# RWKV6 attention and an MLP mixer: the first batch in a fixed order, with more zero products on TensorE

## The chip, the core and the metric

The kernel runs on one core of one Trainium2 chip. The engines that matter are TensorE (PE: matmul; its weight loads are listed as PEld), VectorE (DVE), ScalarE (ACT), GpSimd (POOL) and SyncE (SP), which issues nearly all DMAs. The metric is device time in microseconds, the median of several executions. Everything is float32.

## The reference

For each batch (B = 4), head (H = 8) and time step t (S = 768 steps, head dimension D = 48), the attention keeps a 48 x 48 state:

```
y[t]  = r[t] @ (state + outer(u * k[t], v[t]))
state = w[t][:, None] * state + outer(k[t], v[t])
```

The heads' outputs, side by side, are x of shape (4, 768, 384). The mixer then mixes over tokens and over channels:

```
h   = relu(x^T @ w_tok1) @ w_tok2        # w_tok1 768 x 256, w_tok2 256 x 768
u   = x + h^T
out = u + relu(u @ w_ch1) @ w_ch2        # w_ch1 384 x 1536, w_ch2 1536 x 384
```

The weights come in as 64-bit floats, and the kernel turns them into float32 itself.

## The kernel before, in words

**Attention.** The work is cut into twelve units, three for each batch; a unit is 256 tokens of all heads. Two heads lie on top of each other in the partitions (P = 64 rows each, 48 of them used), and A = 4 such pairs and UC = 2 chunks of 128 tokens lie along the free dimension. Within blocks of 64 tokens the decayed products of r and k are built level by level. `levels(i)` does this for unit i. Its piece `begin` makes copies of r and k with u applied (ScalarE, L195 and L199). `first_block` multiplies in the first decays (`join`, L250 to L252, VectorE), makes the first products on TensorE (`gram0`, L211) and picks the entries that are wanted out of PSUM (`pick0`, L217). `block(l)`, for levels 1 to 5, makes the products (`gram`, L225), joins, and picks (`pick`: VectorE at L234 for levels 1 to 3, ScalarE at L242 for 4 and 5). r and k are changed in place, so a join waits for the gram of its own level, and the next gram waits for the join. The products go to a PSUM pool of two buffers (`ps_g`).

`post(i)` finishes a unit. `tokens(c)` transposes k (L284), `carry(c)` makes the outer products of k and v (L296) and moves the state on by two blocks (L303 to L306), `before(c)` applies r to the states (L318) and `within(c)` adds the products inside the blocks (L331) and copies the result to x (L334). `carry`, `before` and `within` use the one buffer of `ps_a` in turn. The last two pieces load the inputs of unit i + 3 (`load_rkw`, L101, and `load_v`, L108): r, k and w lie in three sets of buffers.

**Weights.** `convert` (L142) loads a piece of a weight matrix as 64-bit words (L149, two buffers), takes the magnitude of the high words on ScalarE (L155) and puts the float32 together in six steps on VectorE (L156 to L161). There are 3 pieces of w_tok1 and 9 of w_ch1, 512 wide, and 4 of w_tok2 and 12 of w_ch2, 384 wide.

**Mixer.** `mixing(bt)` gives the pieces of a batch: `hidden` (L353, two sums that are open over all six chunks), `back` (L360, added to x at L362), `turn` (transposes, L367), `up` (L375, relu at L377) and `down` (L384, sum at L388, then the store at L389). They use the two buffers of `ps_m`. For the first batch `down` of the first segment is cut into pieces of two columns of weights each, with both sums open at once.

**Order.** Pieces are functions with an assumed cost. `woven` merges lists of them by their share of cost done, and `emit` calls them in turn. What a piece emits is then put in order by the framework, which plans each engine's queue by its own estimate of when instructions become ready, with the order of emission as priority: an instruction that is ready may be planned ahead of one that was emitted earlier. So pieces of batch 1 can stand in a queue between those of batch 0.

Of the kernel before, what the change touches and what calls it, by code (L numbers as in the profile page):

```python
# [10 lines left out]
f32 = mybir.dt.float32  # L11
# [31 lines left out]
    return [(c, f) for *_, c, f in sorted(keyed, key=lambda e: e[:3])]  # L43


def emit(pieces):
    for _, f in pieces:
        f()


@with_exitstack
def rwkv6_then_mixer(
    ctx: ExitStack,
# [20 lines left out]

    nc = tc.nc
    pe, dve, act, pool, sp = nc.tensor, nc.vector, nc.scalar, nc.gpsimd, nc.sync

    const = ctx.enter_context(tc.tile_pool(name="const", bufs=1))
    wts = ctx.enter_context(tc.tile_pool(name="wts", bufs=1))
# [29 lines left out]

    u_col = const.tile([128, A], f32, name="u_col")  # L110
    act.dma_start(u_col, u)
    load_rkw(0)
    load_rkw(1)

    masks = []
    for l in range(4):
        b = 1 << l
        m = const.tile([128, 64 // b, 2 if l == 0 else b], f32, name=f"mask{l}")  # L120
        pool.memset(m, 1.0)
        pool.affine_select(out=m, in_=m, compare_op=ALU.is_ge, fill=0.0, base=0,
                           pattern=[[-2 * b, 64 // b], [0, m.shape[2]]], channel_multiplier=1)
        pool.affine_select(out=m, in_=m, compare_op=ALU.is_ge, fill=0.0, base=b - 1,
                           pattern=[[2 * b, 64 // b], [1 if l == 0 else 0, m.shape[2]]], channel_multiplier=-1)
        n, x = (T, 1) if l == 0 else (32, UC * A)
        m8 = const.tile([128, x, n], u8, name=f"mask8_{l}")
        flat = m.rearrange("p n b -> p (n b)")
        for j in range(2):
            dve.tensor_copy(m8[ts(j, T)], flat[ts(j, T), ts(j, n)].unsqueeze(1).to_broadcast([T, x, n]))  # L130
        masks.append(m8)
    for i, t in enumerate(weights_at):
        (dve if i == 0 else pool).memset(t, 0.0)
    ident = const.tile([128, 128], f32, name="ident")
    make_identity(nc, ident)

# [38 lines left out]
    def levels(i):  # L175
# [94 lines left out]
    def post(i):  # L270
# [4 lines left out]
        def tokens(c):  # L275
            if half == 0 and c == 0:
                xs[bt] = xpool.tile([128, C, DM], f32, name="x")
            L = live[i]
            if bt == 0:
                ps = ps_g.tile([128, 2, 512], f32, name="gram")[:, 0, :].rearrange("p (a t) -> p a t", a=A)  # L280
            else:
                ps = ps_m.tile([128, A, 128], f32, name="kT_ps", tag="m")
            for a in range(A):
                pe.transpose(ps[:, a, :], k_[:, ts(c * A + a, 128)], ident)  # L284
            L["kT"] = apool.tile([128, A, 128], f32, name="kT")
            act.copy(L["kT"], ps)

        def carry(c):
            L, vt = live[i], vs[i]
            ch = half * UC + c  # L290
            last = ch == C - 1
            kv = ps_a.tile([128, 2, 512], f32, name="kv_ps", tag="a")
            for a in range(A):
                for j, q in ((0, 0), (1, 1), (0, 1), (1, 0)):
                    if not (last and j == 1):
                        pe.matmul(kv[ts(q, P), j, ts(a, D)], L["kT"][ts(j, T), a, ts(q, P)],  # L296
                                  vt[ts(j, T), c, ts(2 * a + q, D)], start=True, stop=True)
            for j in range(1 if last else 2):
# [173 lines left out]
```

## Time and profile before

| | us |
|---|---|
| median of 3 runs | 690.39 (689.81 to 694.6) |
| the profiled execution | 687.6 |
| its span, first to last instruction | 685.6 |
| PE busy | 641.6 (94%) |
| DVE busy | 293.1 (43%) |
| ACT busy | 194.8 (28%) |

The costliest groups are the channel mixing's two products: L375 203.2 us and L384 198.6 us of PE, followed by the grams at L225, 85.2 us. One matmul of the program is two records in the profile. Busy time of a group overlaps with its neighbours at the edges, and ends of matmuls are modelled. In a timeline row the columns are start, duration, engine, line, operation, output <- inputs, tile sizes and count; in brackets stands the idle time of the engine before it and what ended it. A row can stand for several instructions in a run.

### The profile page before, as it was taken

How to read it: one execution, taken by the hardware profiler on the slowest of the kernel's cores; microseconds unless marked ns; L12 is line 12 of the kernel's file. 1: busy time of each engine (PE TensorE's matmuls, PEld its weight loads, DVE VectorE, ACT ScalarE, POOL GpSimd, SP SyncE). 2: the span in 40 equal slices, each digit the busy share in tenths (PEclk: the TensorE clock that was granted, in tenths of full speed). 3: DMA queues.
4: the chain of work that ended last, by engine and by line, in shares of the span. 5: the costliest groups of instructions: out<-in, count | busy, mean ns of one | idle time of the engine just before them, and what ended most of it. 6: DMA issues, size and time to landing. Idle time of an engine off the chain costs nothing.

```text
span 685.6 us, 18835 instructions
## 1 busy us (share of the span) xinstructions
PE 641.6 (94%) x8584; PEld 466.9 (68%) x8584; DVE 293.1 (43%) x585; ACT 194.8 (28%) x489; POOL 7.2 (1%) x32
## 2 busy tenths in 40 slices
PE   3889998996799999999999999999999999999998
PEld 3877656863586666788677656788677655786854
DVE  5998899998821435442242305442132211000000
ACT  7144533441242123432321303432211201220200
POOL 3000000000000000000000000000000000000000
PEclk9997898998899999999999999999999999999999
DMA  9244544332202131110210312000000000000000
GB/s 345 69 107 132 146 140 126 124 115 71 70 25 81 36 95 48 25 25 5 80 35 3 94 35 60 2 2 2 13 13 2 25 12 12 1 0 12 12 16 31
DMA packets 16111, 38.56 MB, mean 56 GB/s; under 512 B 2176, under 2 KB 8320, under 8 KB 16032
## 3 DMA queue, kind: packets, MB, share of 16 engines
q1 hardware_dynamic: 15888, 37.36, 17.9%
q8 instruction: 67, 1.10, 0.7%
q14 instruction: 12, 0.10, 0.0%
q10 hardware_dynamic: 144, 0.00, 0.0%
HBM read 32.64 MB, written 4.72 MB: 54 GB/s over the span
## 4 chain that ended last, share of the span: by engine, by line
PE 87%; DVE 9%; issue 2%; ACT 1%; DMA 1%; SPq 0%; DVEq 0%; ACTq 0%
PE z_ps L375 29%; PE h_ps L384 28%; PE gram L225 9%; PE h_ps L353 5%; PE h_ps L360 5%; PE y_ps L331 4%; PE kv_ps L296 2%; PE y_ps L318 2%; DVE r L251 1%; DVE k L250 1%; PE kT_ps L284 1%; PE gram L211 1%; PE xT_ps L367 1%; DVE at L217 1%; DMA w<-in_rkw_dram 1%
## 5 line engine op out<-in xcount | busy, mean ns | idle before, releaser
L375 PE MATMUL z_ps<-xT,wch 128*128 128x256 f32 x864 | 203.2, 389 | 3.5 <-DVE wch L161 3.0
L384 PE MATMUL h_ps<-wch,z 128*128 128x384 f32 x576 | 198.6, 498 | 3.7 <-DVE wch L161 3.5
L375 PEld LDWEIGHTS z_ps<-xT,wch 128*128 128x128 f32 x864 | 161.4, 192 | 28.4 <-DVE wch L161 3.2
L384 PEld LDWEIGHTS h_ps<-wch,z 128*128 128x128 f32 x576 | 107.9, 192 | 73.1 <-DVE wch L161 3.7
L377 ACT ACTIVATE z<-z_ps 128x256 f32<-128x256 f32 x144 | 55.1, 383 | 177.3 <-PE z_ps L375 177.2
L225 PEld LDWEIGHTS gram<-r,k 48*64 48x64 f32 x3840 | 76.5, 152 | 34.7 <-issue 24.3
L225 PE MATMUL gram<-r,k 48*64 48x32 f32 x3840 | 85.2, 235 | 13.1 <-DVE r L251 8.5
L388 DVE TENSOR_TENSOR o<-x,h_ps 128x384 f32<-128x384 f32 x24 | 13.3, 554 | 181.9 <-PE h_ps L384 181.9
L250 DVE TENSOR_TENSOR k<-k,decay 112x512 f32<-112x512 f32 x36 | 24.9, 691 | 62.2 <-PE gram L225 62.2
L242 ACT COPY at<-gram 16x256 f32<-16x256 f32 (+1 forms) x72 | 31.2, 434 | 44.7 <-PE gram L225 37.3
L250 DVE TENSOR_TENSOR k<-k,w 112x512 f32<-112x512 f32 x36 | 24.8, 688 | 39.6 <-PE gram L225 32.9
L360 PE MATMUL h_ps<-h,wtok 128*128 128x384 f32 x96 | 36.0, 503 | 1.8 <-DVE x L362 1.8
L353 PE MATMUL h_ps<-x,wtok 128*128 128x384 f32 x96 | 37.0, 520 | 0.0
L331 PEld LDWEIGHTS y_ps<-vt,at 64*64 64x64 f32 x768 | 26.2, 142 | 9.9 <-ACT seen L324 6.3
L234 DVE COPY_PREDICATED at<-mask,gram 128x512 f32<-128x512 uint8 x36 | 32.3, 897 | 0.0
L251 DVE TENSOR_TENSOR r<-r,w 112x512 f32<-112x512 f32 x36 | 24.7, 686 | 16.5 <-ACT rp L195 16.5
L331 PE MATMUL y_ps<-vt,at 64*64 64x48 f32 x768 | 29.2, 227 | 2.1 <-ACT seen L324 1.8
L211 PE MATMUL gram<-rp,kp 48*64 48x64 f32 x768 | 20.1, 246 | 11.1 <-ACT kp L199 8.0
L211 PEld LDWEIGHTS gram<-rp,kp 48*64 48x64 f32 x768 | 17.1, 154 | 16.4 <-ACT kp L199 10.4
L217 DVE COPY_PREDICATED at<-mask,gram 128x512 f32<-128x512 uint8 x24 | 16.7, 725 | 25.7 <-PE gram L211 25.4
L155 ACT ACTIVATE size<-d 128x384 f32<-128x384 f32 (+1 forms) x28 | 17.0, 608 | 28.2 <-DMA d<-in_w_ch_dram 13.3
L324 ACT COPY seen<-y_ps 64x2 f32<-64x2 f32 x44 | 6.8, 154 | 63.6 <-PE y_ps L318 63.3
(50 smaller groups left out, 429.1 us busy)
## 6 DMA issues: line engine op xcount, KB each, us to landing
vt<-in_v_dram SPq DMA_DIRECT2D x12, 384.0 KB, 3.9
d<-in_w_ch_dram SPq DMA_DIRECT2D x9, 512.0 KB, 3.6
d<-in_w_ch_dram SPq DMA_DIRECT2D x12, 384.0 KB, 3.0
out_dram<-o SPq DMA_DIRECT2D x24, 192.0 KB, 1.9
w<-in_rkw_dram SPq DMA_DIRECT2D x18, 192.0 KB, 3.5
k<-in_rkw_dram SPq DMA_DIRECT2D x18, 192.0 KB, 3.5
r<-in_rkw_dram SPq DMA_DIRECT2D x18, 192.0 KB, 3.4
r<-in_rkw_dram SPq DMA_DIRECT2D x3, 512.0 KB, 6.1
```

The source lines that it names most:

```text
L211: pe.matmul(g[cols, q, ts(a, T)], L["kp"][rows, tokens], L["rp"][rows, tokens], start=True, stop=True)
L225: fours(lambda q, j, rows, cols: pe.matmul(g[cols, q, ts(ca, 32)], k_[rows, ds(ca * 128 + j * T, T)], right[rows, ts(2 * ca + j, 32 // b), ...
L234: dve.copy_predicated(out=dst, data=g.rearrange("p q (m b) -> p q m b", b=b), mask=masks[l].rearrange("p x t -> p (x t)").rearrange("p (m ...
L242: act.copy(at[p:p + b, :, :, n * 2 * b + b:(n + 1) * 2 * b], g[p:p + b, :, :, ts(n, b)])
L250: dve.tensor_mul(left, left, wv[:, :, 1].unsqueeze(2).to_broadcast([ROWS, n, b]))
L251: dve.tensor_mul(right, right, wv[:, :, 0].unsqueeze(2).to_broadcast([ROWS, n, b]))
L331: pe.matmul(y[ts(j, T), q, ts(a, D)], at[ts(j, T), q, c * A + a, :], vt[ts(j, T), c, ts(2 * a + q, D)], start=(2 * ch + j == 0 and a == A ...
L353: pe.matmul(sums[i], wtok1[:, c, ts(i, 128)], xs[bt][:, c, :], start=(c == 0), stop=(c == C - 1))
L360: pe.matmul(ps, wtok2[:, i, ts(c, 128)], h1[:, i, :], start=(i == 0), stop=(i == DTOK // 128 - 1))
L375: pe.matmul(ps, wch1[:, m, ts(jt, 128)], xT[:, m, ts(s, SEG)], start=(m == 0), stop=(m == DM // 128 - 1))
L377: act.activation(zs[s][:, jt, :], ps, AF.Relu)
L384: pe.matmul(ps, zs[s][:, jt, ts(n, 128)], wch2[:, jt, :], start=(jt == 0), stop=(jt == NJ - 1))
```

## The change

The first batch, with its attention, weight conversions and token mixing up to most of the first `down`, is emitted with `fixed=True`. `emit` then ties each instruction of PE, DVE, ACT and SP to the one emitted before it on the same engine, so that the framework can't plan it elsewhere; POOL isn't tied. Instructions emitted later without `fixed` are tied behind the last fixed one of their engine, and free among themselves.

The first batch's order is a list: the levels of its three units (a, b, c) start one after the other and alternate; `busy(n)` stands between them, n products of a zeroed part of the wtok2 buffer with itself, 128 x 128 by 256 columns, whose result nobody reads. Then come the pieces of `post`, the hidden pieces and the conversions of w_tok1 and of half of w_tok2, one by one. Updating the states is a piece of its own (`update`), behind the transposes of the next chunk. The loads of units 3 to 5 (`p0[10:]`, `p1[10:]`, `p2[10:]`) are emitted after token mixing and the third piece of w_ch1. The masks are made in one fixed piece ahead of everything, in two shared buffers, and the memset of the first weights_at buffer belongs to that piece. `touched` is a small ScalarE operation at the start; `decay` has three buffers. The diff, cut where it says nothing more:

```diff
-def emit(pieces):
-    for _, f in pieces:
-        f()
...
+    last = {}
+
+    def emit(pieces, fixed=False):
+        for _, f in pieces:
+            done = len(block.instructions)
+            f()
+            for ins in block.instructions[done:]:
+                if ins.engine in (pe.engine, dve.engine, act.engine, sp.engine):
+                    if ins.engine in last:
+                        tc.add_manual_dep(ins, last[ins.engine], behind, reason="order of the pieces")
+                    if fixed:
+                        last[ins.engine] = ins.name
...
+    touched = const.tile([1, 2], f32, name="touched")
+    dve.memset(touched, 0.0)
+    act.mul(touched[:, 1:], touched[:, :1], touched[:, :1])
     load_rkw(0)
     load_rkw(1)
...
+            m = wide.tile([128, 512], f32, name="size", bufs=2)[:, :64 // b * width].rearrange("p (n b) -> p n b", b=width)
...
+    emit([(0, make_masks)], fixed=True)
...
-            decay = apool.tile([128, COLS // 2], f32, name="decay")
+            decay = apool.tile([128, COLS // 2], f32, name="decay", bufs=3)
...
-        pieces = []
-        for c in range(UC):
-            pieces += [(0.5, lambda c=c: tokens(c)), (0.5, lambda c=c: carry(c))]
+        pieces = [(0.5, lambda: tokens(0)), (0.5, lambda: carry(0)), (0.5, lambda: tokens(1)), (0.1, lambda: update(0)),
+                  (0.5, lambda: carry(1)), (0.1, lambda: update(1))]
...
-    emit(woven(levels(0), levels(1)))
-    load_v(0)
     load_rkw(2)
-    load_v(1)
-    load_v(2)
+    for i in range(3):
+        load_v(i)
+
+    def busy(n):
+        ps = ps_m.tile([128, 256], f32, name="busy", tag="m")
+        for _ in range(n):
+            pe.matmul(ps, wtok2[:, 0, :128], wtok2[:, 0, :256], start=True, stop=True)
+
+    dve.memset(wtok2[:, 0, :256], 0.0)
+    a, b, c = levels(0), levels(1), levels(2)
     p0, p1, p2 = post(0), post(1), post(2)
-    p1[4:4] = hiddens[0] + hiddens[1]
-    p2[4:4] = hiddens[2] + hiddens[3]
-    emit(woven(levels(2), p0 + p1, to_tok1))
-    emit(woven(p2[:-4], to_tok2[:2]))
-    emit(p2[-4:-2] + hiddens[4] + p2[-2:] + hiddens[5])
+    begin = [e.pop(0) for e in (a, b, c)]
+    h, t1, t2 = hiddens, to_tok1, to_tok2
+    order = [begin[0], 12, begin[1], a[0], 2, a[1], 2, b[0], 2, a[2], 1, b[1], 2, begin[2], a[3], 2, b[2], 2, c[0], 2,
+             a[4], 2, b[3], 2, c[1], 2, a[5], 2, b[4], 1, c[2], 1, p0[0], b[5], 1, p0[1], c[3], p0[2], p0[3], 1,
+             p0[4], p0[5], 1, p0[6], c[4], p0[7], t1[0], p1[0], p0[8], c[5], p0[9],
+             p1[1], p1[2], *h[0], p1[3], p1[4], *h[1], p1[5], p2[0], p1[6], t1[1], p1[7], p2[2], p1[8], p1[9],
+             p2[1], p2[3], *h[2], p2[4], p2[5], *h[3], p2[6], t1[2], p2[7], p2[8], p2[9], t2[0], *h[4], t2[1], *h[5]]
+    emit([(0.4 * e, lambda e=e: busy(e)) if isinstance(e, int) else e for e in order], fixed=True)
...
-            emit(woven(turned, to_tok2[2:] + to_ch1[:3]))
+            emit(woven(turned, to_tok2[2:] + to_ch1[:3]) + p0[10:] + p1[10:] + p2[10:], fixed=True)
             both = [f for e in zip(ups[0], ups[1]) for f in e]
-            emit(woven(both, to_ch1[3:] + to_ch2[:6]))
-            emit(woven(downs[0][:-4], to_ch2[6:]))
+            emit(woven(both, to_ch1[3:] + to_ch2[:6]), fixed=True)
+            emit(woven(downs[0][:-4], to_ch2[6:]), fixed=True)
```

More of the change, by code (lines that the diff above doesn't have):

```diff
@@ L76, in rwkv6_then_mixer @@
     pe, dve, act, pool, sp = nc.tensor, nc.vector, nc.scalar, nc.gpsimd, nc.sync
+    block = nc.cur_bb.bb
+    behind = mybir.DependencyInfo(mybir.DependencyClass.NoSync, mybir.DependencyReason.DATA)
+    last = {}
[9 more added lines that the diff above has]
+                        last[ins.engine] = ins.name
     const = ctx.enter_context(tc.tile_pool(name="const", bufs=1))
@@ L117, in rwkv6_then_mixer, with make_masks @@
     masks = []
[L118 to L133, printed above, removed]
+    def make_masks():
+        for l in range(4):
+            b = 1 << l
+            width = 2 if l == 0 else b
+            m = wide.tile([128, 512], f32, name="size", bufs=2)[:, :64 // b * width].rearrange("p (n b) -> p n b", b=width)
+            pool.memset(m, 1.0)
+            pool.affine_select(out=m, in_=m, compare_op=ALU.is_ge, fill=0.0, base=0,
+                               pattern=[[-2 * b, 64 // b], [0, width]], channel_multiplier=1)
+            pool.affine_select(out=m, in_=m, compare_op=ALU.is_ge, fill=0.0, base=b - 1,
+                               pattern=[[2 * b, 64 // b], [1 if l == 0 else 0, width]], channel_multiplier=-1)
+            n, x = (T, 1) if l == 0 else (32, UC * A)
+            m8 = const.tile([128, x, n], u8, name=f"mask8_{l}")
+            flat = m.rearrange("p n b -> p (n b)")
+            for j in range(2):
+                dve.tensor_copy(m8[ts(j, T)], flat[ts(j, T), ts(j, n)].unsqueeze(1).to_broadcast([T, x, n]))
+            masks.append(m8)
+        for i, t in enumerate(weights_at):
+            (dve if i == 0 else pool).memset(t, 0.0)
+    emit([(0, make_masks)], fixed=True)
     ident = const.tile([128, 128], f32, name="ident")
@@ L284, in tokens @@
                 pe.transpose(ps[:, a, :], k_[:, ts(c * A + a, 128)], ident)
-            L["kT"] = apool.tile([128, A, 128], f32, name="kT")
-            act.copy(L["kT"], ps)
+            L["kT", c] = apool.tile([128, A, 128], f32, name="kT")
+            act.copy(L["kT", c], ps)
         def carry(c):
@@ L291, in carry @@
             last = ch == C - 1
-            kv = ps_a.tile([128, 2, 512], f32, name="kv_ps", tag="a")
+            kv = L["kv"] = ps_a.tile([128, 2, 512], f32, name="kv_ps", tag="a")
             for a in range(A):
@@ L295, in carry, with update @@
                     if not (last and j == 1):
-                        pe.matmul(kv[ts(q, P), j, ts(a, D)], L["kT"][ts(j, T), a, ts(q, P)],
+                        pe.matmul(kv[ts(q, P), j, ts(a, D)], L["kT", c][ts(j, T), a, ts(q, P)],
                                   vt[ts(j, T), c, ts(2 * a + q, D)], start=True, stop=True)
-            for j in range(1 if last else 2):
+        def update(c):
+            L = live[i]
+            ch = half * UC + c
+            kv = L.pop("kv")
+            for j in range(1 if ch == C - 1 else 2):
                 g = 2 * ch + j
```

## The prediction

> **What bounds the kernel now.** I read the table of stretches first, then TensorE's and VectorE's timelines inside the first 186 us, then the chain and the DMA landings. The stretches (columns: us, then busy us and instruction count of PE, PEld, DVE, ACT, POOL, then granted clock, DMA share, GB/s):
>
> ```profile
> 0.00:38.40 38.40, 24.60 (x772) 22.86 (x772) 29.37 (x57) 18.67 (x46) 6.32 (x24) 1.00 0.57 204
> 38.40:85.30 46.90, 41.90 (x1090) 33.32 (x1090) 40.82 (x91) 21.34 (x55) 0.33 (x3) 0.85 0.45 124
> 85.30:108.00 22.70, 17.78 (x253) 11.40 (x252) 21.93 (x43) 9.13 (x20) 0.00 (x0) 0.97 0.39 123
> 108.00:147.00 39.00, 38.99 (x186) 31.20 (x186) 36.41 (x71) 14.87 (x35) 0.00 (x0) 0.93 0.45 133
> 147.00:185.90 38.90, 27.84 (x595) 17.89 (x594) 34.49 (x72) 8.99 (x19) 0.00 (x0) 0.87 0.24 71
> 185.90:254.00 68.10, 66.75 (x878) 47.48 (x874) 20.48 (x45) 19.13 (x50) 0.33 (x3) 1.00 0.23 63
> ```
>
> Up to 185.9 us VectorE is the full engine (163 of 186 us); afterwards TensorE has no gap worth naming and VectorE is below a third. So the total is: TensorE's work, plus what TensorE loses before 186 us. What paces the early part is weight conversion, six dependent VectorE steps:
>
> ```profile
> 112.12 0.42 DVE L156 TENSOR_SCALAR cut<-d 128x512 uint32<-128x512 uint32 x1
> ...
> 115.29 0.69 DVE L161 SCALAR_TENSOR_TENSOR wch<-size,scale 128x512 f32<-128x512 f32 x1
> 115.90 0.42 DVE L156 TENSOR_SCALAR cut<-d 128x512 uint32<-128x512 uint32 x1
> ```
>
> One 512-wide conversion back to back is 115.90 - 112.12 = 3.78 us; a 384-wide one, read the same way (131.01 to 134.12), is 3.11 us. TensorE's timeline shows it waiting for them, and what its clock does:
>
> ```profile
> 27.46 3.89 PE L225 MATMUL gram<-r,k 48*64 48x32 f32 x128 [0.37 <-DVE at L234]
> ...
> 100.59 1.14 PE L225 MATMUL gram<-r,k 48*64 48x32 f32 x64 [0.22 <-DVE r L251]
> ...
> 108.01 13.28 PE L375 MATMUL z_ps<-xT,wch 128*128 128x256 f32 x48 [2.34 <-DVE wch L161]
> 123.09 10.63 PE L375 MATMUL z_ps<-xT,wch 128*128 128x256 f32 x48
> ...
> 156.00 1.56 PE L384 MATMUL h_ps<-wch,z 128*128 128x384 f32 x4 [2.10 <-DVE wch L161]
> ```
>
> Sixty-four gram records take 1.95 us at 27 us and 1.14 at 100: TensorE is slow in the first 40 us although the clock column says 1.00 there. And in 75 to 186 us the queues carry grams (L211, L225) of batch 1 between the conversions of batch 0: VectorE's form groups give 12 first-level picks (L217) and 32 left products (L250) before 190 us, where batch 0 alone needs 6 and 18.
>
> **What the Trainium skill says.** "TensorE: Matmul & The Clock Gate", Part 1: the array runs at half clock until a 3.4 us window has been busy, and falls back after an idle one. The trace agrees (1.95 against 1.14 us; 0.50 granted between 48.6 and 55.3 us) and adds that a stream of small grams, 93% busy in the records from 25 to 35 us, does not release it. "PSUM — Partial Sum Buffer", Engine vs sequencer instructions: the queues of ScalarE and VectorE are strict FIFO, so a fixed order is what runs, stalls included; nothing in this trace contradicts it, though none of its rows tests it. "DMA: Bandwidth & Descriptors", Queues, rings and completion order: each engine consumes a ring in order. The trace's start agrees: 6.95 MB were queued, and landings grow with position.
>
> ```profile
> r<-in_rkw_dram SPq DMA_DIRECT2D x3, 512.0 KB, 6.1
> k<-in_rkw_dram SPq DMA_DIRECT2D x3, 512.0 KB, 6.9
> w<-in_rkw_dram SPq DMA_DIRECT2D x3, 512.0 KB, 7.6
> vt<-in_v_dram SPq DMA_DIRECT2D x3, 384.0 KB, 9.8
> d<-in_w_tok_dram SPq DMA_DIRECT2D x2, 512.0 KB, 11.0
> ```
>
> A lone weight load of 512 KB takes 3.6 us.
>
> **The change, part by part.** Call the attention units of batch 0 a, b, c; a level is a gram, two products (L250, L251: 1.20 us by start-to-start), the next decay (0.6 down to 0.1) and a pick (1.22, 1.08, 0.6, 0.6; the last two on ScalarE). A unit is 12.2 us of VectorE.
>
> *Masks, memset, table load.* The mask casts (8 instructions, 2.2 us of VectorE at 8.4 to 11.6) move ahead of the first product, into VectorE's idle time up to 7.16 us; the memset (0.9) moves behind them, so the first product starts at about 7.9. Worth -1.5 us. POOL's mask work now shares two buffers and so waits for a cast or two (0.3 us each); it ended at 6.4 us, so this stays in the same idle time. The table load, at 1.23 us already, was hidden by the first DMA: 0. load_v(0) goes behind load_rkw(2) on SP: a first use at 46 us hides it. The third decay buffer: 0, what it lets start earlier stands behind other work in the fixed order.
>
> *Products of zeros.* One is two records of 256 columns: 10.63/48 = 0.22 each, 0.44 us warm, 0.85 cold. Twelve while the first loads arrive, from about 1.5 us: five to seven cold, the rest warm, ending at 8.5 to 9.7, against a first gram at 7.96 now; that gram then takes 1.5 instead of 2.3 us, so 0 net. The other 28 are 12.4 us of TensorE warm. Between 30 and 45 us TensorE's own sum (five grams of 1.2, products 4.9 us, a transpose) is as long as VectorE's, so here they are partly on the path.
>
> *Levels.* Grams have two buffers, freed by picks, and the order is fixed, so I wrote it out piece by piece: a1 must wait for its gram with nothing behind it (1.45 us), b0's second gram waits for a1's pick, a4, b3, c2 and b5 wait 0.4 to 1.3 us each. Through the third level of c that is 30.7 us of VectorE plus 6 of waits: 7.9 + 36.7 = 44.6. Before, at 46.6 us, VectorE had done two units, c's first products, unit 0's states and a conversion. So no gain.
>
> *Posts.* carry, before and within share one accumulator (kv_ps, y_ps). A unit is twice (kv 0.66, update 4 x 0.39, release 0.2) and twice (y 0.68, seen 0.4, within 1.1, copy 0.55): 10.3 us. From 46: unit 0 takes 14.5 because c3 to c5 stand between, unit 1 11, unit 2 to its last update 4.7: 76.2. Behind that, in VectorE's order, stand t1[2], t2[0], t2[1] (3.78 + 2 x 3.11): the first back() at X = 86.2. Now it is at 85.4. Bounds: 82 (no wait beyond data) to 91 (half clock returns in the posts).
>
> *Token mixing.* VectorE's fixed order: first back 1.7, two wtok2 conversions 6.2, three wch1 11.3, six additions of 0.5: 22.2. The third wch1 conversion ends at 108.4; now at 107.96.
>
> *The moved loads.* load_rkw(3..5) and load_v(3..5) leave the posts and stand in SP's order behind the load of wch1's third piece, ahead of its fourth: 18 x 192 KB + 3 x 384 KB = 4.72 MB. The page gives 37.36 MB in 17.9% of the span, 304 GB/s: 15.5 us. They start when wch1's first piece has been read (X + 12.4 = 98.6), drain at 114.1, and the fourth piece behind them lands at 117.7 (1.7 for itself, 1.9 fixed); it is wanted at 108.4. Stall 9.3; at the 410 GB/s of the start 4.9; 0 if the queue doesn't hold it back. I take 8. Queued behind it: all later conversions on VectorE, and on ScalarE the abs (L155) of that piece with the relus of the ups after it, so TensorE too.
>
> *Conversions.* Six of wch1 and twelve of wch2 follow with nothing between: 22.7 + 37.3 = 60.0. The last ends at 108.4 + 8 + 60.0 = 176.4, downs[0] at 178.4 (two column products). Now it is 185.9: **-7.5**. Before that, ups[2] can't start: downs[0] holds both ps_m buffers.
>
> *The debt.* The grams of batch 1 are now behind all fixed pieces. Before 185.9 the old order had run 704 records of L225 and 192 of L211 of them; at later rates (40.3/2156 and 8.8/384 us) 17.6, less 4% overlap 16.9, less one gram0 that can still run in the wait: **+15.4**. From 186 us on TensorE is the bound, so this is paid in full. Batch 1's chain of 18 levels and three posts, some 70 us alone, must now hide in 90 us of TensorE work: +1, from 0 to 9. The split of carry and update in later batches: 0, within 1 either way.
>
> **Sum.** -7.5 + 15.4 + 1.0 = +8.9 on the profiled execution's 687.6 us (span 685.6, 2.0 around it): 696.5. That execution is 2.8 below the median of the runs, 690.39, which gives 699.3. I say 698.
>
> **Rivals.** Everything hangs on when the fourth wch1 conversion starts: 116.4 here, and each us of it is a us of the total.
> - *The loads don't hold it back* (they are spread, or the weight load passes): it starts at 108.4 to 110. The DMA share of 0.39 to 0.45 speaks for it, the landings above against. 691.
> - *Faster.* VectorE, free of batch 1, runs dense through the first 80 us: its sum there is 36.6 + 17.6 + 8 of states = 62 us from 7.9. If eight of my sixteen us of waits are not there (warm products, alternation) and the loads hide, the conversion starts at 98 and the total is 680. It decides from 100.6 on. Against it: the single accumulator.
> - *Much slower.* The exposed chain of batch 1 (9) and half clock in the posts (5): 711. For: TensorE waited for L250 and L251 at 241 to 243 us already now, with most levels done.
>
> **Chances.** 698: 0.48; 691: 0.23; 680: 0.13; 711: 0.16. Three quarters of the first lie over 1% (6.9 us, about what a measurement here can tell): slower 0.36 + 0.16 = 0.52; same 0.12 + 0.23 = 0.35; faster 0.13. The range leaves out the faster case and the tail of the worst: 684 to 710.
>
> **What would show it.** Sixty-four gram records at 1.14 us from 12 us on (clock); first back() near 86; a VectorE gap before the fourth wch1 conversion, put down to d (L149) with landings over 10 us; no L217 of batch 1 before the last wch2 conversion; ups[2] at 178; TensorE dense after. A first back() before 78 us, or no gap, makes it wrong.

## The result, and the profile after

The changed kernel takes **724.43 us** (median of four runs, 714.84 to 732.47), the kernel before 690.10 on the same chip: 1.040 times as long, 95% interval 1.028 to 1.052. Runs more than 1.5% above the fastest of their kernel are left out of every ratio in this document, though not out of the medians. The direction was forecast, the size was not: 698 was said, with 710 as the upper end. The profiled execution is the shortest run, 714.84 us (span 713.1), where the working had 696.5. The other runs are longer by up to 17.6 us, at lower granted clocks (.971 in the shortest, .932 in the longest); the last group of experiments is about that.

The stretches of the changed kernel are cut at the first `back`, the end of the third wch1 conversion, the start of the fourth, the start of the third segment's `up` and the first hidden product of batch 1; columns as before:

```profile
0.00:38.40 38.40, 32.60 (x786) 25.59 (x788) 29.45 (x55) 14.06 (x36) 6.55 (x24) 1.00 0.48 184
38.40:91.20 52.80, 45.69 (x1054) 35.39 (x1046) 35.18 (x76) 17.75 (x43) 0.33 (x3) 0.81 0.12 35
91.20:113.75 22.55, 14.20 (x47) 7.48 (x46) 20.17 (x38) 6.19 (x12) 0.00 (x0) 0.91 0.63 171
113.75:128.65 14.90, 4.71 (x14) 3.62 (x14) 0.01 (x2) 0.38 (x1) 0.00 (x0) 0.73 1.02 260
128.65:192.90 64.25, 51.26 (x302) 35.72 (x302) 59.53 (x116) 25.89 (x65) 0.00 (x0) 0.96 0.35 108
192.90:282.00 89.10, 84.09 (x1695) 61.35 (x1695) 48.40 (x96) 26.86 (x70) 0.33 (x3) 0.98 0.20 58
```

Two rows matter. In the fourth, 14.9 us long, VectorE does nothing at all while the DMA engines are full. In the second, VectorE is busy 35.2 of 52.8 us, where the kernel before had 40.8 of 46.9. The timelines of the changed kernel show what stands in these two. First the gap, on SP (which issues the loads), VectorE and TensorE:

```profile
95.81 7.88 SPq L167 DMA_DIRECT2D d<-in_w_ch_dram  x3
103.74 0.89 SPq L112 DMA_DIRECT2D r<-in_rkw_dram  x2
...
120.04 0.39 SPq L119 DMA_DIRECT2D vt<-in_v_dram  x1
121.79 59.80 SPq L167 DMA_DIRECT2D d<-in_w_ch_dram  x18
```

```profile
113.06 0.69 DVE L179 SCALAR_TENSOR_TENSOR wch<-size,scale 128x512 f32<-128x512 f32 x1
128.65 0.43 DVE L174 TENSOR_SCALAR cut<-d 128x512 uint32<-128x512 uint32 x1 [14.89 <-DMA d<-in_w_ch_dram]
```

```profile
116.53 1.99 PE L397 MATMUL z_ps<-xT,wch 128*128 128x256 f32 x8
129.70 9.61 PE L397 MATMUL z_ps<-xT,wch 128*128 128x256 f32 x34 [11.17 <-ACT z L399]
```

The fourth wch1 load goes out at 121.8 us, behind all 21 moved loads, and VectorE starts on it at 128.65. TensorE's wait is put down to ScalarE's relu (L399). That relu stands in ScalarE's fixed order behind the abs of the missing piece (L173), so the cause is the load:

```profile
115.07 0.38 ACT L399 ACTIVATE z<-z_ps 128x256 f32<-128x256 f32 x1 [3.55 <-PE z_ps L397]
128.71 0.67 ACT L173 ACTIVATE size<-d 128x512 f32<-128x512 f32 x1 [13.25 <-DMA d<-in_w_ch_dram]
129.27 0.65 ACT L399 ACTIVATE z<-z_ps 128x256 f32<-128x256 f32 x2
```

Now the early part, TensorE:

```profile
11.98 1.14 PE L243 MATMUL gram<-r,k 48*64 48x32 f32 x64
...
60.80 1.90 PE L243 MATMUL gram<-r,k 48*64 48x32 f32 x64
62.49 1.92 PE L354 MATMUL y_ps<-vt,at 64*64 64x48 f32 x32
...
73.00 1.14 PE L354 MATMUL y_ps<-vt,at 64*64 64x48 f32 x32 [0.47 <-ACT seen L347]
```

With the zero products 64 grams take 1.14 us at 12 us, the time that they take at full clock; inside the posts the clock is at half again (0.50 granted from 51.9 to 69.0 us). VectorE ends the last state update of the third unit at 80.7 us:

```profile
80.37 0.35 DVE L329 TENSOR_TENSOR state<-state,kv_ps 128x192 f32<-128x192 f32 x1 [0.54 <-PE kv_ps L314]
```

### The profile page after: what moved, and what is told of

Its sections match the earlier page's. It is cut to its first block, busy times and chain, and to the rows that moved or that the text cites. A ratio compares the mean times of both kernels' runs of the same rounds, so it can differ in the third digit from the quotient of the medians.

```text
span 713.1 us, 18995 instructions
## 1 busy us (share of the span) xinstructions
PE 655.5 (92%) x8664; PEld 471.3 (66%) x8664; DVE 301.1 (42%) x587; ACT 193.8 (27%) x490; POOL 7.4 (1%) x32
## 3 DMA queue, kind: packets, MB, share of 16 engines
q1 hardware_dynamic: 15888, 37.36, 17.1%
HBM read 32.64 MB, written 4.72 MB: 52 GB/s over the span
## 4 chain that ended last, share of the span: by engine, by line
PE 79%; DVE 12%; DMA 5%; ACT 2%; issue 2%; SPq 0%; DVEq 0%; ACTq 0%
PE h_ps L406 24%; PE z_ps L397 24%; PE gram L243 8%; PE h_ps L375 5%; PE h_ps L382 4%; PE y_ps L354 4%; DMA d<-in_w_ch_dram 2%; PE busy L438 2%; PE y_ps L341 2%; PE kv_ps L314 2%; DVE k L268 2%; DVE r L269 1%; PE kT_ps L302 1%; PE gram L229 1%; DMA vt<-in_v_dram 1%
## 5 line engine op out<-in xcount | busy, mean ns | idle before, releaser
L397 PE MATMUL z_ps<-xT,wch 128*128 128x256 f32 x864 | 207.7, 393 | 16.9 <-ACT z L399 14.5
L406 PE MATMUL h_ps<-wch,z 128*128 128x384 f32 x576 | 195.3, 492 | 7.1 <-DVE wch L179 6.6
L399 ACT ACTIVATE z<-z_ps 128x256 f32<-128x256 f32 x144 | 54.4, 381 | 167.8 <-PE z_ps L397 167.7
L243 PEld LDWEIGHTS gram<-r,k 48*64 48x64 f32 x3840 | 65.1, 137 | 26.6 <-issue 17.5
L243 PE MATMUL gram<-r,k 48*64 48x32 f32 x3840 | 72.3, 223 | 7.3 <-DVE r L269 3.1
L268 DVE TENSOR_TENSOR k<-k,decay 112x512 f32<-112x512 f32 x36 | 25.0, 694 | 66.1 <-PE gram L243 64.5
L173 ACT ACTIVATE size<-d 128x384 f32<-128x384 f32 (+1 forms) x28 | 16.9, 607 | 46.7 <-DMA d<-in_w_ch_dram 44.0
L382 PEld LDWEIGHTS h_ps<-h,wtok 128*128 128x128 f32 x96 | 16.4, 189 | 15.9 <-DVE x L384 2.7
L438 PE MATMUL busy<-wtok 128*128 128x256 f32 x80 | 25.6, 454 | 1.3 <-DVE wtok L440 1.3
```

The lines of the kernel that those rows point to most:

```text
L243: fours(lambda q, j, rows, cols: pe.matmul(g[cols, q, ts(ca, 32)], k_[rows, ds(ca * 128 + j * T, T)], right[rows, ts(2 * ca + j, 32 // b), ...
L268: dve.tensor_mul(left, left, wv[:, :, 1].unsqueeze(2).to_broadcast([ROWS, n, b]))
L382: pe.matmul(ps, wtok2[:, i, ts(c, 128)], h1[:, i, :], start=(i == 0), stop=(i == DTOK // 128 - 1))
L397: pe.matmul(ps, wch1[:, m, ts(jt, 128)], xT[:, m, ts(s, SEG)], start=(m == 0), stop=(m == DM // 128 - 1))
L399: act.activation(zs[s][:, jt, :], ps, AF.Relu)
L406: pe.matmul(ps, zs[s][:, jt, ts(n, 128)], wch2[:, jt, :], start=(jt == 0), stop=(jt == NJ - 1))
```

## Experiments

All times are medians beside the kernel before on the same chip. The table holds landmarks of the profiled executions, in us: the first `back`; VectorE's start on the fourth wch1 piece; the first `up` of the third segment (ups[2]); the first hidden product of batch 1; the span. From that hidden product to the end every kernel in it needs 429.6 to 431.2 us, so what a profiled execution costs is decided by then.

| kernel | back | 4th wch1 | ups[2] | hidden | span |
|---|---|---|---|---|---|
| before | 85.3 | 107.9 | 185.9 | 254.8 | 685.6 |
| changed | 91.2 | 128.7 | 192.9 | 282.0 | 713.1 |
| loads_back | 100.0 | 125.1 | 189.9 | 279.0 | 710.2 |
| sp_free | 92.0 | 114.1 | 178.3 | 267.0 | 698.2 |
| front_only | 91.7 | 124.1 | 216.0 | 280.3 | 711.3 |
| before_fix_mix | 88.3 | 110.9 | 174.7 | 264.5 | 695.4 |
| early_levels | 93.2 | 116.4 | 182.6 | 260.4 | 689.9 |
| unfixed | 98.0 | 107.2 | 184.6 | 261.1 | 692.0 |
| no_zero | 92.7 | 130.0 | 195.6 | 286.5 | 717.6 |
| spread_no_zero | 92.8 | 117.1 | 185.0 | 274.9 | 706.1 |

### The moved loads

**loads_back**: each unit's loads back behind its own post, the order fixed as in the changed kernel.

```diff
-... p0[8], c[5], p0[9],
+... p0[8], c[5], p0[9], *p0[10:],
...
-            emit(woven(turned, to_tok2[2:] + to_ch1[:3]) + p0[10:] + p1[10:] + p2[10:], fixed=True)
+            emit(woven(turned, to_tok2[2:] + to_ch1[:3]), fixed=True)
```

(and the same for p1 and p2)

> One edit on the changed kernel: the loads of units 3, 4 and 5 stand again behind each unit's last within, the rest stays fixed. Theory 'burst' (the 4.7 MB in a row hold back the fourth piece of w_ch1): VectorE's gap of 14.9 us ahead of that conversion falls below 1 us, ups[2] starts at 178 instead of 193, and the profiled time falls by 13 to 15 us, to about 700. Rival 'clock' (half clock in TensorE's windows sets the time, the gap only stands where VectorE has nothing to do anyway): the gap goes, but the time falls by less than 5 us. Rival 'loads early hurt': the twelve DMAs delay the loads of w_tok1 and w_tok2, and the first back() comes 3 us or more later than 91.2.

712.71 us, ratio 1.029 (1.023 to 1.035). The gap ahead of the fourth wch1 piece is gone, yet the profiled execution gains only 2.9 us, and `back` comes 8.8 us later, as the third theory said. In the fixed queue of SP the weight loads now stand behind loads that wait until a unit's buffers are read. VectorE's largest idle time has moved ahead of the second wtok2 conversion:

```profile
96.68 0.36 DVE L174 TENSOR_SCALAR cut<-d 128x384 uint32<-128x384 uint32 x1 [8.40 <-DMA d<-in_w_tok_dram]
```

**sp_free**: the pieces stand as in the changed kernel; SP alone isn't tied.

```diff
-                if ins.engine in (pe.engine, dve.engine, act.engine, sp.engine):
+                if ins.engine in (pe.engine, dve.engine, act.engine):
```

> The changed kernel with SP alone taken out of the engines whose order is fixed; the pieces stand where they stood. If the burst of loads of units 3 to 5 costs what its stall shows, the gap of 14.9 us ahead of the fourth wch1 conversion is under 5 us, the first product of the second mixing stage stays near 91 us, the first product of the third segment (ups[2]) comes near 180 to 184 us and not at 192.9, and the kernel is 8 to 12 us shorter than the changed one at the same clock (about 705 to 714). Rival, that loads put early hurt whoever places them: the first product of the second stage moves to 96 or later, as with the loads put back by hand, and the time stays at 711 or more. Rival, that the debt of batch 1 rules: the gap goes, ups[2] comes 10 us earlier, but the first product of batch 1's hidden stage still comes 89 us after it.

703.30 us (699.95 to 706.48), ratio 1.016 (1.009 to 1.022). VectorE goes from the third to the fourth piece without a pause:

```profile
110.28 0.42 DVE L174 TENSOR_SCALAR cut<-d 128x512 uint32<-128x512 uint32 x1
114.06 0.42 DVE L174 TENSOR_SCALAR cut<-d 128x512 uint32<-128x512 uint32 x1
```

ups[2], the hidden product and the end all come 14.6 to 14.9 us earlier, the length of the gap (14.9), though `back` is 0.8 later. That line alone is the largest part of the 27.5 us between the two spans.

**loads_spread**: SP fixed as in the changed kernel, the loads written one at a time between the conversions.

```diff
-            emit(woven(turned, to_tok2[2:] + to_ch1[:3]) + p0[10:] + p1[10:] + p2[10:], fixed=True)
+            first = woven(turned, to_tok2[2:] + to_ch1[:3])
+            first[4:4], first[8:8] = p0[11:], p0[10:11]
+            emit(first, fixed=True)
...
-            emit(woven(both, to_ch1[3:] + to_ch2[:6]), fixed=True)
+            second = woven(both, to_ch1[3:] + to_ch2[:6])
+            for n, e in zip((24, 20, 12, 8), (p2[11], p2[10], p1[11], p1[10])):
+                second.insert(n, e)
+            emit(second, fixed=True)
```

> The changed kernel with all its fixed order, SP's too, but the loads of units 3 to 5 written piece by piece between the conversions (one unit's or one v load at a time) in place of all together behind the third wch1 conversion. If the stall is the burst itself, six loads that the next weight load must let pass, no idle of VectorE over 5 us stands in the conversions, the second stage stays at 91 us, the last wch2 conversion ends at 172 to 180 us against 189, the first hidden product of batch 1 comes at 265 to 272, and the time is 700 to 708, as with SP free (703.3). If SP's fixed order costs by itself, wherever the loads stand, the last conversion ends after 185 and the time is 711 or more.

717.03 us, ratio 1.021 (1.008 to 1.034), with runs from 703.95 to 725.53. The two at the highest clocks, 703.95 and 705.71, are where the first theory had them. The profile fell on a run with a clock of .947, so its landmarks can't be set beside the table's; but in it, too, the fourth piece starts 3.77 us after the third, without a pause. The kernel with the same loads and no zero products (below) shows it at a clock of .983: 3.78 us, and VectorE waits no longer than 1.71 us for a weight load up to 135 us. So the gap came from the burst, 21 loads in one place, and not from the fixing of SP as such.

### The fixed mixing and the work of batch 1

**before_fix_mix**: the kernel before, with only the conversions (from the third piece of w_tok2 on), `turned`, `ups` and the first `downs` of batch 0 fixed; `emit` as in the changed kernel.

```diff
-            emit(woven(turned, to_tok2[2:] + to_ch1[:3]))
+            emit(woven(turned, to_tok2[2:] + to_ch1[:3]), fixed=True)
...
-            emit(woven(both, to_ch1[3:] + to_ch2[:6]))
-            emit(woven(downs[0][:-4], to_ch2[6:]))
+            emit(woven(both, to_ch1[3:] + to_ch2[:6]), fixed=True)
+            emit(woven(downs[0][:-4], to_ch2[6:]), fixed=True)
```

> The kernel before with one part of the change alone: the conversions, turned, ups and the first downs of batch 0 in fixed order; the attention of batch 0 and its loads as before. My working of this part: second stage at 85 us, third wch1 conversion at about 108, no burst of loads (they went out in the posts), ups[2] 7 to 13 us earlier than before (173 to 179 us), batch 1 shut out until then, its first hidden product 85 to 89 us after ups[2], at 258 to 268 against 254.8 before: time 693 to 704. Rival, that the fixed order alone gives the whole loss: ups[2] at 186 or later and the time 710 or more. Rival, that it gains: the first hidden product of batch 1 before 253 and the time 680 to 688.

696.44 us, ratio 1.007 (1.005 to 1.010). ups[2] is 11.2 us earlier and the hidden product 9.8 later: 89.8 us from one to the other, against 68.8 before. Wherever the mixing is fixed and batch 1 kept out, this distance is nearly the same: 89.1, 89.1, 88.8, 90.9 and 89.9 us in the changed kernel, loads_back, sp_free, no_zero and spread_no_zero. So the debt, as the prediction called what batch 1 still has to do, is 20 to 22 us each time, and it is made good only as far as the conversions end earlier.

**early_levels**: before_fix_mix, with the levels of batch 1's first unit written into batch 0's last post, free to be moved.

```diff
-    emit(woven(p2[:-4], to_tok2[:2]))
+    emit(woven(p2[:-4], to_tok2[:2], levels(UB)))
...
-            att = levels(n)
+            att = [] if n == UB else levels(n)
```

> The kernel before with the mixing of batch 0 fixed (as in before_fix_mix) and one thing more: the levels of batch 1's first unit are written into batch 0's last post, free to be moved, ahead of the fixed part. If what the fixed mixing costs is the batch-1 work that it shuts out of VectorE's idle time (21.6 us busy of 40 between 50 and 90 us, 34.2 in the kernel before), that work comes back: VectorE over 30 us busy between 50 and 90, the last wch2 conversion at 170 to 176 us and the first hidden product of batch 1 at 248 to 256 us against 264.5, time 680 to 692. Rival, that the loss is of the fixed order among the conversions themselves: hidden at 262 or later, time 695 to 700. Rival, that the level work delays the second stage by what it fills: second stage at 95 or later, time 692 to 700.

691.36 us, ratio 1.000 (0.997 to 1.003): the loss of before_fix_mix is gone. VectorE's stretch from 50 to 90 us, in before_fix_mix and then here:

```profile
50.00:90.00 40.00, 36.45 (x723) 27.36 (x724) 21.61 (x50) 11.65 (x31) 0.22 (x2) 0.83 0.49 130
```

```profile
50.00:90.00 40.00, 35.94 (x1096) 28.71 (x1093) 33.42 (x72) 14.90 (x39) 0.22 (x2) 0.94 0.44 121
```

VectorE does 11.8 us more in this stretch, about what the fixed mixing had left idle there (the kernel before has 34.2 busy). The distance from ups[2] to the hidden product falls to 77.7 us. The hidden product, at 260.4, is later than expected (248 to 256): the second stage also moved, by 4.9 us, in the direction of the second rival. The time is right and the mechanism half of it.

**unfixed**: the changed kernel with every `fixed=True` taken out; sequence, zero products, masks and late loads stay.

```diff
-    emit([(0, make_masks)], fixed=True)
+    emit([(0, make_masks)])
```

(and so in the other four places)

> The changed kernel with every fixed order taken away: the same pieces written in the same sequence, engines free to be reordered. If the fixing is what costs, the first product of the second stage comes at 85 to 88 us, batch 1's levels run between the conversions as before, and the time is 688 to 698. If the sequence itself costs, as in the run with the mixing alone left free (727.5 us), the first product of the second stage comes at 90 or later, ups[2] after 200, and the time is 715 to 730. Early grams and zero products should stand as written or close to it in both.

694.00 us, ratio 1.002 (0.999 to 1.004): no loss that can be measured. Yet `back` comes at 98.0, later than in the changed kernel: the first theory's landmark was wrong and its time right. VectorE is 76.8 us busy up to 91 us here, 75.4 in the kernel before, 64.5 in the changed one; what it does meanwhile is conversions and levels of batch 1. In this comparison an early `back` isn't what counts; how full VectorE is goes with the time.

**mix_free**, **loads_back_mix_free** and **front_only**: the opposite case, the attention part fixed and the mixing free (with the loads behind the mixing; with the loads back in the posts; with SP free).

```diff
-            emit(woven(both, to_ch1[3:] + to_ch2[:6]), fixed=True)
-            emit(woven(downs[0][:-4], to_ch2[6:]), fixed=True)
+            emit(woven(both, to_ch1[3:] + to_ch2[:6]))
+            emit(woven(downs[0][:-4], to_ch2[6:]))
```

(and `turned` with the first conversions likewise)

> Only fixed is taken away from token mixing, ups and downs; the loads stay emitted behind token mixing. The queue is then free to issue loads that are ready ahead of weight loads that wait for a buffer. 'Burst': if the loads are planned early, VectorE's gap goes and the time is within 4 us of the run with both edits; if they stay in one row, a gap of 5 to 15 us stays and the time is 700 to 705. 'Debt': in either case below the changed kernel by 12 us or more.

> The loads as in the first of these runs, and token mixing, the first two ups and the first downs are emitted without fixed, so grams of batch 1 may stand between the conversions again; the first batch's attention stays in its written order. Theory 'debt' (fixing the mixing shuts batch 1 out of TensorE's waits, some 17 us of grams have to be made up while TensorE is the bound, and its chain is exposed for another 5): 10 to 18 us below the run with the loads alone moved back, 684 to 690, level with the kernel before within 1%. Rival 'written order of the attention' (the first 91 us are the loss): stays over 695.

> The changed kernel with the fixed order left in the attention part alone and there for TensorE, VectorE and ScalarE only: SP is free and the conversions, turned, ups and downs are free. If the parts add up (703.3 with both fixed and SP free; 696.4 with the mixing fixed alone, 4.6 over the kernel before), the fixed front costs some 7 us: 697 to 701, the second stage at 90 to 93 us. If instead the free mixing behind a fixed front is what made 727.5 us with SP fixed, the conversions stretch past 210 us, ups[2] starts after 215 and the time is 715 to 730. Rival, that the front costs nothing once SP is free: 690 to 694.

727.53, 726.34 and 719.35 us; ratios 1.051 (1.042 to 1.059), 1.050 (1.043 to 1.056) and 1.033 (1.027 to 1.040). My theory that the fixed mixing alone makes the debt, so that freeing it would bring 684 to 690, fell here. front_only starts its second stage at the time of sp_free, and VectorE is as far behind by then (65 us busy in the first 91). The free mixing then lets batch 1's levels in at once, while the conversions are still to be done: 960 records of L243 between 90 and 235 us, against 704 in unfixed, and the last step of the last conversion starts at 213.8 us against 173.8 in sp_free. TensorE waits for weights until 214 us (two groups of TensorE in front_only, 90 to 235 us):

```profile
L406 PE MATMUL h_ps<-wch,z 128*128 128x384 f32 x48 | 24.4, 649 | 8.3 <-DVE wch L179 8.3
L243 PE MATMUL gram<-r,k 48*64 48x32 f32 x960 | 23.1, 243 | 9.9 <-DVE r L269 9.4 <-DVE at L235 0.5
```

So the parts don't add up, and not because of the loads. Why free planning costs 3.3 to 5.1% behind a fixed front and nothing in `unfixed` is only partly shown: the 11 us of VectorE that the fixed front loses are there in sp_free too, and cost less in it.

**front_free**: SP and the attention free, the mixing fixed.

```diff
-    emit([... for e in order], fixed=True)
+    emit([... for e in order])
```

> The changed kernel with SP free and the attention of batch 0 in its written sequence but not fixed; the mixing of batch 0 fixed on TensorE, VectorE and ScalarE. If the parts add up (703.3 with the front fixed as well; 696.4 for the kernel before with the mixing alone fixed; 694.0 with nothing fixed), it comes to 695 to 699, with the first hidden product of batch 1 at 263 to 267. If the fixed front is worth nothing beside a fixed mixing, it stays at 702 to 705. Rival, that a free front takes batch-1 work into VectorE's gaps and ends at 690 to 694: that asks for VectorE over 30 us busy between 50 and 90.

706.03 us, ratio 1.023 (1.013 to 1.034), with clocks of .946 to .963: not shorter than sp_free (.959 to .976). The expected gain of some 7 us from freeing the front didn't come; what freeing it is worth at the same clock isn't shown.

**sp_free_levels**: sp_free, with the levels of batch 1's first unit written by hand into the order, and the loads of unit 3, which they need, moved up into it.

```diff
-... p0[9],
+... p0[9], *p0[10:],
...
-... p2[6], t1[2], p2[7], p2[8], p2[9], t2[0], *h[4], t2[1], *h[5]]
+... p2[6], d[0], t1[2], p2[7], p2[8], d[1], p2[9], t2[0], d[2], *h[4], t2[1], d[3], *h[5]]
...
+            emit(woven(turned, to_tok2[2:] + to_ch1[:3], d[4:]) + p1[10:] + p2[10:], fixed=True)
```

> The changed kernel with SP free and the levels of batch 1's first unit written by hand into the order, from the third post to the first conversions of wch1. If shut-out batch-1 work is the rest of the loss, the first hidden product of batch 1 comes at 252 to 260 us against 267.0 with SP free alone, time 688 to 697. Rival, that the fixed order makes the written levels wait for their loads or makes the posts wait for them: second stage later than 98 us, conversions ending later than 185, time 700 or more.

704.96 us, ratio 1.022 (1.018 to 1.026): the rival. `back` moved to 101.4, the fourth wch1 piece to 130.1, the hidden product to 272.6. Of the 9.4 us that `back` comes later than in sp_free, 3.8 stand before VectorE reaches the first of the written pieces, in a run whose clock was at half from 24.5 to 34.8 us already. The other 5.6 come in behind them. The levels that were free to fall into idle time in early_levels delay what stands behind them when they are fixed.

### The zero products and the clock

**no_zero**: the changed kernel with all but one of the zero products left out (nobody reads their results).

```diff
-        for _ in range(n):
+        for _ in range(min(n, 1) if n == 12 else 0):
```

> The changed kernel without its products of zeros but one; the order is otherwise as it was. 'Clock' (the products hold TensorE at full clock through the levels, and that is what they are for): 64 gram records take 1.9 to 2.0 instead of 1.14 us up to 40 us, and the first back() comes 2 to 6 us later than 91.2; the total follows one for one. My own working: the products cost as much on TensorE's path between 30 and 45 us as the clock gives back, so the first back() stays within 2 us of 91.2 and the time within 1% of the changed kernel.

719.18 us (716.53 to 720.19), ratio 1.038 (1.032 to 1.045). TensorE's grams run at half speed from the start, where the changed kernel had 1.14 us:

```profile
11.99 1.93 PE L243 MATMUL gram<-r,k 48*64 48x32 f32 x64 [1.79 <-DVE at L235]
```

and yet `back` is only 1.4 us later, which fits the working: what the zero products gain in the grams they mostly cost themselves. The span is 4.5 us longer; why another 3 us come in behind the fourth wch1 piece isn't shown.

**zeros_in_posts**: seven more zero products between the first posts' pieces.

```diff
-... c[2], 1, p0[0], b[5], 1, p0[1], c[3], p0[2], p0[3], 1,
-             p0[4], p0[5], 1, p0[6], c[4], p0[7], t1[0], ...
+... c[2], 1, p0[0], b[5], 5, p0[1], c[3], p0[2], p0[3], 2,
+             p0[4], p0[5], 2, p0[6], c[4], p0[7], 1, t1[0], ...
```

> The changed kernel with seven more products of zeros (some 5 us of TensorE at half clock, 2.4 at full) between the pieces of the first posts, where its clock fell to half at 52.6 us. If the half clock there is what put the second stage at 91.2 us, the small products of 52 to 70 us run at full clock (64 grams in 1.14 us, not 1.9), the second stage begins at 86 to 88 us and the kernel is 3 to 5 us shorter at the same clock. Rival, that the idle waits on VectorE's states and ScalarE's copies set that time: the second stage stays at 90 to 92 us and the time is within 1% of the changed kernel's 714.8 to 732.

729.14 us, three runs near 729 and one of 713.54: no gain shown. In its profiled run the clock was at half from 18.6 to 66.4 us, so the run is no test of the expectation as it stood. From 66.4 us on, though, the clock was full to the end of the posts, and they were hardly shorter: from the third level of c to unit 2's last state update VectorE took 35.0 us, with 6.9 of them at half clock, against 35.4 in the changed kernel, with 17.1 at half clock. That speaks against half clock as the whole of what the posts lost; but the seven products stand in that stretch as well, and the cause stays open.

**spread_no_zero** (loads_spread with the edit of no_zero) and **after_again** (the changed kernel unaltered), on one chip:

> The changed kernel with the loads spread between the conversions (as in loads_spread) and all products of zeros but one taken out. If the zero products are what puts some runs 12 to 22 us above the shortest (loads_spread 704 to 725.5 with clocks .976 to .929, the changed kernel 714.8 to 732.5 with .971 to .932, against 716.5 to 720.2 with .971 to .978 without them), all runs lie within 6 us of each other, at 704 to 710, with a clock of .965 or more. If the fixed order's pauses lower the clock by themselves, runs of 715 and more with clocks under .95 come here too.

> The changed kernel unaltered, on the same chip beside the other. If the products of zeros bring the spread, its runs again reach from about 714 to over 728, with clocks from .97 down to .93 and the longer runs at the lower clocks; if the first four runs were a chance, they lie within 6 us at 714 to 720.

708.87 us, with six runs from 707.82 to 711.03 and clocks of .978 to .983; ratio 1.026 (1.022 to 1.030). The changed kernel beside it: 719.96 us, six runs from 715.11 to 733.66 with clocks of .968 to .928; ratio 1.039 (1.034 to 1.044). In ten runs without the zero products (this kernel and no_zero) none strays by more than 2.7 us from its median; with them, and the front fixed, the changed kernel's ten span 19 us. The zero products alone don't do it: `unfixed` has them, and its 20 runs lie between 690.1 and 697.7 at .960 or more. Nor do zero products and a fixed front bring it each time: loads_back and sp_free_levels have both, and their four runs each lie within 1.7 us. And the kernel before, which has none, spans 13.1 us in seven runs on one chip (685.08 to 698.17). So the zero products aren't shown to be what spreads the runs; what does is open. The difference of spread_no_zero to no_zero, 10.3 us, is the burst of loads once more, in kernels with a steady clock. No version here beats the kernel before by what can be measured; early_levels and unfixed come level with it.

## Why the prediction was wrong

The step that failed is the size of the stall by the moved loads: it was put at 8 us and measured 14.9. The attention ahead of it was 5.0 us too short and the debt 3.9, and the lower clock of the other runs had no term. Right were the direction and the mechanisms of the stall and of the debt. The sum was 18.3 us short on the profiled execution (696.5 against 714.84). The median then lies 9.6 us above that execution, where 2.8 were allowed; the two together are the 25.1 us between the 699.3 of the working and 724.43. Step by step, as measured:

- **Masks** (said: first product at 7.9): VectorE's casts waited for POOL until 4.70 us and the first product came at 9.38. 1.5 us short; I had put POOL's mask work into idle time. The levels made up part of it: the third level of c ended at 45.3, where 44.6 was said.
- **Products of zeros** (said: net 0): near it for `back`, which comes 1.4 us later without them in no_zero. That the runs could spread as they do had no place in the sum: the median lies 9.6 us above the shortest run in the first four, 4.9 in the six later ones.
- **Levels and posts** (said: `back` at 86.2, bounds 82 to 91): 91.2. The 5.0 us are nearly all in the posts. From the third level of c to unit 2's last state update 31.6 us were counted (44.6 to 76.2); they took 35.4, to 80.7. I had put the bound of 91 down to half clock in the posts, and the timeline shows half clock there (1.90 us for 64 grams, where 1.14 was counted). That it makes these 3.8 us isn't shown: zeros_in_posts needed 35.0 us with far less of it. I took the middle although the kernel before already had 0.50 granted at 48.6 to 55.3 us.
- **Token mixing** (said 22.2): 22.55.
- **The moved loads** (said 8): **14.9**, the largest miss. The mechanism was as forecast: queue order, what stands behind it on VectorE, ScalarE and TensorE. The size was missed three times. The burst took 18.1 us on SP (103.74 to 121.79), 261 GB/s for the 4.72 MB where I used 304, the mean of the kernel before on its profile page. The fourth piece took 6.9 us from its issue to VectorE's start instead of 3.6, with the DMA engines full all along (1.02). And I took 8 where the working gave 9.3. sp_free confirms the term: 14.6 to 14.9 us return everywhere behind it.
- **Conversions** (said 60.0): 60.4. From their end to ups[2] 4 us instead of 2.
- **The debt** (said 15.4 and 1 exposed): 89.1 - 68.8 = 20.3. With the 15.4 as worked out, 4.9 us are left for the exposed chain, inside my 0 to 9 but not 1. The stretches agree: TensorE stood idle for 5.0 us between ups[2] and the hidden product (84.09 busy of 89.10), against 1.4 before (66.75 of 68.10). The distance came again in before_fix_mix.

Together: 5.0 at `back`, 0.3 in token mixing, 6.9 in the gap, 2.3 in and behind the conversions, 3.9 in the debt: 18.4. Of the rivals, the loads that don't hold back (691) and the faster one (680) were refuted by the gap and by `back` at 91.2. The much slower one (711) had a later `back` and an exposed chain, as measured, and the loads at 8 like the sum; with the 14.9 it would have said 718. Of the signs named, full clock at 12 us, the gap put down to the load and batch 1's picks only behind the last conversion came; a first `back` near 86 and ups[2] at 178 did not.

"PSUM — Partial Sum Buffer" in the Trainium skill, section Engine vs sequencer instructions, was named for strict FIFO queues without a row to test it. The changed kernel has that row, and it agrees: relus whose products were done by 118.5 us wait until 129.27, more than 10 us, behind an abs whose load isn't there.

## What to carry to other kernels

Ahead of fixing an order, ask of each load in it what stands behind it in the issuing engine's queue and how many bytes lie in front: here a burst of 18.1 us that nobody needed yet cost 14.9, since the next load needed was behind it, and leaving SP's order free took that away. Where the planner could move work, it filled the idle time of the bounding engine from elsewhere; the same work written in by hand at a guessed place delayed what followed, and work shut out returned later on an engine that by then was full. When a kernel's runs spread, compare the granted clock of each before explaining the median.

## What the runs showed of the hardware

The clock fell to half, and stayed there, without TensorE being idle for long. In a run of the unaltered changed kernel (727.18 us, clock .94) 0.50 was granted from 31.5 to 82.7 us. In the 17 us from 34 to 51 us of it TensorE was busy all the time. Four records of zero products took 2.07 us instead of 1.13, and 64 grams 1.93 instead of 1.14.

```profile
34.00:51.00 17.00, 17.00 (x322) 12.86 (x324) 8.24 (x16) 3.27 (x8) 0.00 (x0) 0.50 0.01 2
```

```profile
29.60 1.13 PE L438 MATMUL busy<-wtok 128*128 128x256 f32 x4
31.32 1.83 PE L243 MATMUL gram<-r,k 48*64 48x32 f32 x64 [0.59 <-DVE at L235]
33.08 2.07 PE L438 MATMUL busy<-wtok 128*128 128x256 f32 x4
35.08 1.93 PE L243 MATMUL gram<-r,k 48*64 48x32 f32 x64
```

"TensorE: Matmul & The Clock Gate" in the Trainium skill, Part 1, gives an idle window of some 3.4 us as what ends full clock, and a busy one as what brings it back; of one kernel it tells that frequent short pauses made the clock swing. In this run the last pauses before the fall are 1.03 and 0.59 us, so no idle window ended full clock, and 17 us without a pause didn't bring it back. Whether short pauses set it off isn't shown. Elsewhere an idle window is there: in the profiled run of the changed kernel TensorE stood still from 118.5 to 129.7 us, and the grant fell to 0.50 at 123.6. The fall at 48.6 us in the kernel before, which the prediction read as agreeing with the page, had no such window; the longest pause in the 8 us ahead of it was this:

```profile
46.10 0.67 PE L318 MATMUL y_ps<-state,r 48*64 48x48 f32 x16 [1.36 <-DVE state L306]
```

While the clock was down in that run, the products that fill waits were not free: in the fixed order they stood in front of the grams, with no pause between. What sets off the fall wasn't found.
